# Moving the two requests for w_in from SyncE's DMA queue to ScalarE's

## The chip, the cores and the metric

The kernel runs on one NeuronCore of one Trainium2 chip. The core has five engines with one in-order instruction stream each: TensorE (PE, with its weight loads shown as PEld), VectorE (DVE), ScalarE (ACT), GpSimd (POOL) and SyncE (SP). Data come from HBM to the on-chip memory by DMA transfers. A transfer is asked for by an instruction in the stream of one engine, and the core's 16 DMA engines carry it out. The metric is the time of one execution on the device, in microseconds (us).

## The reference

Two stages. The first is a gated linear recurrence over 4 batches, 8 heads, 768 positions and a head size of 48. The second is a gated MLP over the 384 joined head outputs of each position, with a hidden width of 1024.

```python
for t in range(S):
    state = alpha[:, :, t, :, None] * state + np.einsum('bhd,bhe->bhde', k[:, :, t], v[:, :, t])
    y[:, :, t] = np.einsum('bhd,bhde->bhe', q[:, :, t], state)
...
h = np.maximum(x @ w_in, 0.0)                     # x: (4, 768, 384), w_in: (384, 1024)
u, v = (h[..., :d_ff // 2].copy(), h[..., d_ff // 2:].copy())
v_n = (v - mu) / np.sqrt(var + 1e-06)             # over the 512 columns of v
v_s = np.einsum('ts,bsd->btd', w_spatial, v_n) + b_spatial[None, :, None]
return ((u * v_s) @ w_out).astype(np.float32)
```

So w_in has two halves of 384 x 512 numbers: half 0 makes u, half 1 makes v. Each half is 768 KB in float32.

## The kernel before

**Stage one** works on chunks of 128 positions, 24 in all (6 per batch). The first 8 chunks (batch 0 and the first two of batch 1) are done in pairs by `pair` (lines 423 to 632), the rest one by one by `first` (lines 634 to 790). For each pair four loads of 384 KB bring `ac` (alpha), `kc`, `qc` and `vc` (line 441). They move rows of 96 numbers, 384 bytes. From `ac` ScalarE makes logarithms (`la`, line 452). TensorE adds them up (line 461). ScalarE makes the two exponentials (lines 469 and 478). These scale k (`kt`, line 483, on VectorE or GpSimd) and q (`qt`, line 490, on VectorE). TensorE transposes both (line 511), makes scores (line 583), and adds up the output from the masked scores (line 610) and from the running state (line 623). The output is turned into `xT`, the input of stage two.

**Stage two** has `second_v` (lines 867 to 940), which multiplies `xT` with half 1 of w_in, and normalizes. `second_u` multiplies with half 0. `second_s` multiplies with w_spatial, and `second_o` with w_out. All of their matmuls are recorded under the helper's line 828.

**Weights** come through `fetch` (lines 1073 to 1097): one DMA of 768 KB into one of two float32 buffers called `raw_w` (for w_in in rows of 512 numbers, 2 KB), and then casts to bfloat16. For each half of w_in there are three casts: two on GpSimd (line 199) and one on ScalarE (line 197). A third `raw_w` load, of w_spatial, can start only when the casts of half 1 have read their buffer, and the fourth only when those of half 0 have.

**The order of the work** is written out by hand in `PLAN`. Each word is an engine's letter (P, D, A, G, S for TensorE, VectorE, ScalarE, GpSimd, SyncE; Q marks a DMA's own time and issues nothing) and the number of an operation. `replay` (lines 111 to 120) emits the operations in this order, and each engine runs its own in order. A number behind a colon adds a matmul on junk data in front (line 187). The operations that matter here:

- S163, S165, S167, S169: the requests for `ac`, `kc`, `qc`, `vc` of the third pair (chunks 4 and 5). S307, S309, S311: `ac`, `kc`, `qc` of the fourth pair.
- S4 and S9: the requests for half 1 and half 0 of w_in (line 1081). Half 1 stands between `ac` and `kc` of the third pair, half 0 between `vc` of the third and `ac` of the fourth.
- A78: ScalarE's cast of the first chunk's output (`x_sb`, line 197). Next on ScalarE is A108, the cast of the second pair's `vc` (`vbp`).
- A171: ScalarE's logarithm of the third pair's `ac` (line 452). Next on ScalarE is A183, the first exponential of the third pair (line 469).
- A8, G7, G6: the casts of half 1. A13, G11, G12: those of half 0.

Of the kernel before, what the change touches and what calls it, by code (L numbers as in the profile page):

```python
# [61 lines left out]
Q308 P131 P134 D133 D136 D132 D135 G70 G118 P172:228 P182 P123:240 A183 A8 A173 A124 P137 P138 A139 A174 G7 G6 D125  # L62
P85 G126 D128 D185 G127 G129 G175 P88 P142 P140 A86 A184 D176 D186 A143 A89 P188 P190 P180 P144 P178 A141 A191 A145
A181 P146 G11 G12 S309 Q310 S311 Q312 D130 D87 D179 D90 D189 P157 A187 A177 A158 A147 A13 P197 P200 P192 D199 D201
D198 D194 D202 P151:196 P155 A315 A193 A91 P326 P316 A327 P203 P153 P204 G195 G196 G329 A317 A328 A318 P149 A205 A154
D159 D156 D152 D330 G319 P208 P334 A209 P206 D320 P332 P324 P210 P322 D92 D335 D325 D333 D148 A207 P212 A211 A150 P347
P215 P221 A213 A160 A222 A216 S14 Q15 P223 P227 S18 Q19 D93 D323 D161 D348 D349 D214 G16 G17 A224 A228 P225 P229 A226
A21 P232 A234 D231 D230 D233 G20 P235:300 P238 S313 Q314 G331 G321 P344 P336 S367 Q368 S369 Q370 S22 Q23 S371 Q372
A237 A236 D217 D162 D346 A240 D338 A239 A218 D219 D220 A375 A337 P251 P263 P259 P376 A377 A378 G339 P264 D345 D341
D265 P260 D261 P255 P252 A380 A25 A24 D381 D253 P256 D257 G340 G342 G379 S409 Q410 S373 Q374 S446 Q447 S411 Q412 S413  # L70
Q414 S415 Q416 S26 Q27 S480 Q481 S448 Q449 S482 Q483 S450 Q451 S484 Q485 P383 A385 A417 S452 Q453 S577 Q578 S486 Q487
S581 Q582 S579 Q580 S583 Q584 P244 P241 P350 A246 D384 D245 D242 D243 P390 P354 P418 D392 D391 A351 A355 G262 G343
A420 A382 G254 G266 P279 P352 P271 P356 P393 P272 A353 A357 A419 G421 A422 A394 P280 P361 P386 P275 P395 A362 A424
A396 A31 D273 D423 D281 D387 P425 D397 D427 D426 D363 G282 G388 P276 P358 D277 P398 G258 G389 G278 G30 A399 A454 A359
A28 A488 P405 P432 P267 P455 P401 A402 A457 A456 D29 P291 P489 P268 A490 A459 D406 D433 D400 D434 D360 P283 P428 D269
D460 A492 D429 D493 G458 G491 P435 A284 A292 A436 G274 G461 G270 G430 G431 S648 Q649 S617 Q618 S650 Q651 S611 Q612
S652 Q653 S613 Q614 S690 Q691 S615 Q616 S694 Q695 S654 Q655 S692 Q693 P287 P462 P437 P495 P403 D463 D464 D497 D496
A288 A439 A438 P440 A585 A441 A364 D404 P469 P498 P295 P465 P586 P303 D471 D470 D466 D500 D499 A296 A587 A588 A590
A304 P299 G494 G467 G468 G589 G592 D591 D442 P472 A473 P501 P407 P474 A502 A300 P503 P593 P596 A443 A505 A408 D475
D476 P477 A478 D504 D366 D594 D595 D445 D444 D597 D365 P506 P600 P515 D601 D516 A507 A479 A508 D509 D602 A656 A510  # L80
A619 P517 P525 P513 P519 P529 P657 P533 P620 D511 D512 P526 P530 A514 A659 A658 A621 A661 A622 A698 A624 D518 D520
D527 D531 D662 P545 P534 P699 A701 A700 A703 D625 G598 G599 G660 G626 G623 G528 D535 P546 D547 P630 P627 P664 P537
P603 D631 D665 D704 G548 A629 A628 G632 G663 A604 P538 P634 P605 S728 Q729 S762 Q763 S696 Q697 S730 Q731 S732 Q733
S764 Q765 S766 Q767 D539 A607 A666 A606 D635 D636 P541 P667 P542 G702 G532 P706 P671 D668 D543 D673 D672 G669 G536
G670 G544 G633 P608 P637 P521 A707 A736 A708 A638 P737 P713 P639 P522 P549 D714 D715 D641 D523 A770 A609 A705 A738
A739 G740 A640 A741 D742 P771 P550 P642 A772 P709 P744 A774 A643 A746 D710 D551 D775 D745 D644 G524 S858 Q859 S734
Q735 S929 Q930 S860 Q861 G773 G711 G552 G712 G743 G540 P716 P674 A717 A675 P561 P718 P676 P777 P553 A562 A678 A677
D719 D779 D720 D610 P679 P751 A778 A554 A866 A680 A645 A681 P780 D752 P747 D748 D753 D781 D782 P682 P867 P721 P754
A868 A869 A871 A722 A755 S768 Q769 S862 Q863 A723 A776 D683 D872 P573 P688 P684 G749 G750 G870 P756 P874 D646 D757
D875 D685 D758 A689 A574 D724 A876 P686 P783 P569 P881 A784 P785 A570 A787 A687 A725 D882 D786 D883 P759 P557 A760  # L90
P788 P565 P796 P798 P800 S1042 Q1043 S971 Q972 S892 Q893 S864 Q865 S898 Q899 S896 Q897 A979 A558 A789 A566 A937 A900
S894 Q895 S935 Q936 G873 S975 Q976 S931 Q932 S933 Q934 S973 Q974 S977 Q978 S1008 Q1009 S567 Q568 S1046 Q1047 S559 Q560
S1012 Q1013 S1010 Q1011 S1044 Q1045 S1014 Q1015 D727 D647 D761 D726 P794 P806 D790 A791 D799 D797 D795 D792 D793 D801
P901 P980 P802 P938 P877 P807 A902 A903 A907 A905 A981 A939 A940 A982 A944 A984 P810 P803 A942 G904 D878 G941 G879
D808 D906 D804 G805 G880 G809 G983 D985 D943 P822 P884 P811 D812 A885 P823 P908 P886 P945 D824 P814 P911 P815 D912
D909 D816 G813 G817 G913 G825 A910 A887 A888 A947 A946 P889 A1016 A890 P952 P915 P987 D953 D916 D954 P830 P1017 P831
P818 A988 A1019 A1050 A1018 D917 P948 P819 P1051 D949 A1021 A986 A989 D1022 D832 G950 P834 A1052 G951 G1020 P990 P842
P918 A835 A1054 D820 D991 D1055 A843 A919 P838 P1024 P994 P920 D1025 D921 D995 D996 A839 A1023 G914 G833 G1053 G992
S1048 Q1049 S575 Q576 S836 Q837 S844 Q845 S293 Q294 S289 Q290 S571 Q572 S305 Q306 S301 Q302 S555 Q556 A922 A1026 S297
Q298 S285 Q286 S840 Q841 P826 P955 P827 D828 A956 P1057 P957 P1031 D958 P1027 D1028 D1033 D1032 P997 P923 A1058 A1059  # L100
A959 P969 P1060 A1056 A998 P999 D1062 D1001 D1061 D970 G821 G829 G993 G1029 A1000 A924 P960 P846 P1034 A961 A847 G1030
P1063 A1035 A1064 P1002 P963 P1036 P1065 D925 D891 A1003 D962 D1066 P850 P967 A1067 A1037 D1004 A926 D928 P1068 A964
A1038 P1039 D927 D968 A851 A1005 A1069 A1040 D1006 D1041 D1007 D1070 P965 P854 P1076 P1080 P1078 P1074 D966 A1079 A855
A1071 A1081 D1075 D1072 D1073 D1077 P1094 P1082 P1106 P1086 P1083 P1098 P1095 P1090 P1102 P1087 P1107 P1091 P1103
# [19 lines left out]
def kernel(  # L124
# [946 lines left out]
    fetched, casts = [], []  # L1071

    def fetch(key, prio, to, src):

        n, cols = src.shape[1], src.shape[2]
        hold = {}

        def load(_):
# [2 lines left out]
            nc.sync.dma_start(out=hold["w"], in_=src)  # L1081
# [75 lines left out]
```

## Time and profile before

| what | value |
| --- | --- |
| time, median of 3 runs | 146.31 us (146.35, 144.73, 146.31) |
| span of the profiled execution, first to last instruction | 142.7 us (the profile gives this execution no other time) |
| busy, share of the span | PE 94%, DVE 83%, ACT 77%, POOL 58% |
| granted TensorE clock | 1.000 of full speed |
| request for half 1 of w_in | SP, 11.69 us, 8.3 us to landing |
| request for half 0 of w_in | SP, 19.86 us, 7.3 us to landing |
| ScalarE's A78 and A171 | 14.06 to 14.54 us and 17.33 to 18.18 us |

Times in the trace count from the start of the span. An engine counts as busy while an instruction of it runs. The time of a DMA request on SP's line is the time that the instruction held SP, not the time of the transfer. "To landing" goes from the start of the request to the arrival of the last byte.

### The profile page before, as it was taken

What the parts mean: (1) busy time and instruction counts of PE and PEld (TensorE: products, weight loads), DVE (VectorE), ACT (ScalarE), POOL (GpSimd) and SP (SyncE); (2) the same over time, 40 slices, a digit from 0 to 9 for tenths busy, and PEclk for the clock granted to TensorE, in tenths of its full rate; (3) what the DMA queues carried; (4) which work ended last, traced back from release to release, by engine and by line L of the source; (5) the groups of instructions that cost most, each with busy time, mean ns of one, the idle gap of its engine ahead of it and who ended that gap; (6) DMA issues with size and microseconds to landing.
All of it is one profiled execution on the core that took longest, in us unless ns stands there. A gap on an engine that the chain in (4) does not pass through costs nothing.

```text
span 142.7 us, 4968 instructions
## 1 busy us (share of the span) xinstructions
PE 134.7 (94%) x1912; PEld 84.8 (59%) x1923; DVE 118.3 (83%) x291; ACT 109.3 (77%) x282; POOL 83.4 (58%) x146
## 2 busy tenths in 40 slices
PE   7999798899999999999999999999999989999990
PEld 3457575566577656675666665656666656566560
DVE  7279878989989699999998898989979779994940
ACT  3477759999888969889987999997978978940061
POOL 6703977366339776982389999410799993000720
PEclk9999999999999999999999999999999999999999
DMA  4999999999998999999999998999998794113045
GB/s 106 270 261 261 321 259 256 290 289 358 236 217 160 237 226 202 194 169 203 171 196 183 182 198 140 214 152 194 191 231 165 229 341 168 56 58 111 0 161 170
DMA packets 89000, 28.64 MB, mean 201 GB/s; under 512 B 83728, under 2 KB 87440, under 8 KB 88976
## 3 DMA queue, kind: packets, MB, share of 16 engines
q1 hardware_dynamic: 88944, 28.32, 91.3%
q8 instruction: 15, 0.25, 0.8%
q14 instruction: 9, 0.07, 0.2%
q0 software_dynamic: 32, 0.00, 0.0%
HBM read 23.60 MB, written 4.72 MB: 198 GB/s over the span
## 4 chain that ended last, share of the span: by engine, by line
PE 63%; SPq 9%; POOL 7%; DMA 6%; DVE 5%; ACT 4%; issue 3%; ACTq 0%; POOLq 0%; DVEq 0%
PE bank L828 46%; SPq L441 8%; DMA qc<-in_q_dram 6%; PE bank L719 2%; PE bank L754 2%; POOL kt L690 2%; POOL gT L989 2%; POOL sbd L199 2%; PE bank L782 2%; DVE ptm L765 1%; PE bank L740 1%; PE bank L666 1%; SPq L1081 1%; PE bank L776 1%; DVE qt L490 1%
## 5 line engine op out<-in xcount | busy, mean ns | idle before, releaser
L828 PE MATMUL bank<-w_spT,vn 128*128 128x384 bf16 x192 | 36.8, 326 | 0.0
L989 POOL TENSOR_TENSOR gT<-vsb,uT 128x384 bf16<-128x384 f32 x28 | 25.7, 925 | 14.9 <-DVE vsb L976 14.4
L765 DVE TENSOR_TENSOR ptm<-bank,mask 128x512 bf16<-128x512 f32 x32 | 20.7, 682 | 1.9 <-PE bank L398 1.2
L828 PEld LDWEIGHTS <-vn 128*128 128x128 bf16 x192 | 16.6, 97 | 9.5 <-issue 0.2
L690 POOL TENSOR_TENSOR kt<-kc,binv 128x384 bf16<-128x384 f32 x16 | 14.6, 915 | 9.9 <-ACT bc L685 5.1
L976 DVE TENSOR_TENSOR vsb<-bank,bsp_bc 128x384 f32<-128x384 f32 x31 | 16.5, 551 | 4.2 <-PE bank L828 2.5
L828 PE MATMUL bank<-xT,w_in 128*128 128x384 bf16 x96 | 18.7, 326 | 0.0
L828 PE MATMUL bank<-w_out_sb,gT 128*128 128x384 bf16 (+1 forms) x100 | 18.7, 319 | 0.0
L828 PE MATMUL bank<-w_in,xT 128*128 128x512 bf16 x61 | 17.1, 379 | 0.8 <-issue 0.2
L344 POOL TENSOR_TENSOR state<-state,bc 128x192 f32<-128x192 f32 x20 | 10.4, 522 | 8.9 <-ACT bc L559 3.4
L197 ACT COPY kqT<-bank 128x512 bf16<-128x512 bf16 x21 | 12.1, 598 | 3.7 <-PE bank L719 1.1
L199 POOL CAST sbd<-state 64x192 bf16<-64x192 f32 x38 | 13.3, 350 | 2.0
L893 DVE BATCH_NORM_STATS2 stats<-v_sb 128x6 f32<-128x512 bf16 x20 | 13.6, 682 | 0.3 <-ACT v_sb L203 0.3
L203 ACT ACTIVATE v_sb<-bank 128x512 bf16<-128x512 f32 x20 | 11.7, 604 | 1.2 <-PE bank L828 1.0
L828 PEld LDWEIGHTS <-w_in 128*128 128x128 bf16 x96 | 8.8, 97 | 5.9
L828 PEld LDWEIGHTS <-gT 128*128 128x128 bf16 x100 | 8.9, 97 | 5.6 <-DVE gT L989 0.4
L199 DVE COPY kqT<-bank 128x512 bf16<-128x512 bf16 x27 | 10.4, 416 | 1.9 <-PE bank L511 1.0
L197 ACT CAST x_sb<-bank 128x384 bf16<-128x384 f32 x24 | 11.4, 489 | 0.7 <-PE bank L610 0.2
L187 PE MATMUL bank<-junk 128*128 128x512 f32 (+9 forms) x24 | 10.5, 542 | 1.1 <-DVE junk L240 1.1
L197 ACT COPY xT<-bank 128x192 bf16<-128x192 bf16 (+1 forms) x26 | 9.3, 376 | 1.7 <-PE bank L398 1.1
L594 DVE TENSOR_TENSOR ptm<-bank,mask 128x512 bf16<-128x512 f32 x16 | 10.2, 682 | 0.5 <-PE bank L583 0.3
L197 ACT COPY o_sb<-bank 128x384 f32<-128x384 f32 x9 | 4.4, 484 | 8.0 <-PE bank L828 8.0
(126 smaller groups left out, 285.4 us busy)
## 6 DMA issues: line engine op xcount, KB each, us to landing
ac<-in_alpha_dram SPq DMA_DIRECT2D x16, 192.0 KB, 4.4
kc<-in_k_dram SPq DMA_DIRECT2D x16, 192.0 KB, 4.9
qc<-in_q_dram SPq DMA_DIRECT2D x16, 192.0 KB, 4.3
vc<-in_v_dram SPq DMA_DIRECT2D x16, 192.0 KB, 4.4
raw_w<-in_moe_w_spatial_dram SPq DMA_DIRECT2D x3, 768.0 KB, 6.7
out_dram<-raw_w SPq DMA_DIRECT2D x11, 192.0 KB, 2.7
out_dram<-o_sb SPq DMA_DIRECT2D x9, 192.0 KB, 1.9
ac<-in_alpha_dram SPq DMA_DIRECT2D x4, 384.0 KB, 6.2
```

The source lines that it names most:

```text
L187: nc.tensor.matmul(out=flat[:, 0:cols].rearrange("p (a b) -> p a b", a=4), lhsT=junk, rhs=junk[:, None, 0:n].to_broadcast([128, 4, n]), st ...
L197: nc.scalar.copy(out=out, in_=in_)
L199: ENG[eng].tensor_copy(out=out, in_=in_)
L203: nc.scalar.activation(out=out, in_=in_, func=AF.Relu)
L344: ENG[eng].tensor_tensor(out=st["state"], in0=st["state"], in1=st["bc"][:, :, None].to_broadcast([128, HP, D]), op=ALU.mult)
L441: nc.sync.dma_start(out=t.rearrange("p h a d -> p h (a d)"), in_=src[b, :, t0:t0 + 2 * C, :].rearrange("h (p a) d -> p h (a d)", a=2))
L690: ENG[eng].tensor_mul(out=k_blocks(kt3)[:, :, :, 0:D], in0=quad(st["kc"]), in1=st["binv"])
L765: nc.vector.tensor_tensor(out=st["ptm"][:, s], in0=st[f"pt{s}"], in1=mask4, op=ALU.mult)
L828: return lambda ps: nc.tensor.matmul(out=out(ps), lhsT=lhsT(), rhs=rhs(), start=start, stop=stop)
L893: nc.vector.bn_stats(out=stats, in_=d["v_sb"][:, tt, :])
L976: nc.vector.tensor_tensor(out=hold["vs"], in0=ps[:, 0:TH], in1=bsp_bc[:, th, :], op=ALU.add)
L989: ENG[eng].tensor_tensor(out=bt[b]["gT"][:, dsl, cols], in0=hold["vs"], in1=bt[b]["uT"][:, dsl, cols], op=ALU.mult)
```

## The change

Both requests for w_in leave SyncE's stream and go into ScalarE's: half 1 behind A78, half 0 behind A171. They then go out on ScalarE's DMA queue. Buffers, sizes, casts and all other operations keep their places. The rest of `PLAN` is only wrapped anew.

```diff
 PLAN = """
 ...
-S163 Q164 S4 Q5 S165 Q166 S167 Q168 P59:464 G58 G48 A44 A45 A55 D46 D57 D47 P249:304 P49 P61 A50 P51 D52 D60 A62 A102
-A250 P71:304 P74 P113 P103 D72 D73 D76 D75 P63 P77:172 D65 A114 D116 P119:148 A104 A64 A115 A105 A78 G66 G67 G106 D107
-D117 D68 P79 P81 P111 P121 P247 P109 G3 G69 A108 A82 A80 D120 D122 D112 D110 P83 A84 A171 D248 S169 Q170 S9 Q10 S307
+S163 Q164 S165 Q166 S167 Q168 P59:464 G58 G48 A44 A45 A55 D46 D57 D47 P249:304 P49 P61 A50 P51 D52 D60 A62 A102 A250
+P71:304 P74 P113 P103 D72 D73 D76 D75 P63 P77:172 D65 A114 D116 P119:148 A104 A64 A115 A105 A78 A4 Q5 G66 G67 G106
+D107 D117 D68 P79 P81 P111 P121 P247 P109 G3 G69 A108 A82 A80 D120 D122 D112 D110 P83 A84 A171 A9 Q10 D248 S169 Q170
 ...
         def load(_):
             flat = raws.tile([128, n * cols], FP32, name="raw_w")
             hold["w"] = flat.rearrange("p (n f) -> p n f", n=n)
-            nc.sync.dma_start(out=hold["w"], in_=src)
-
-        dma(key, WT, load, list(fetched[-NRAW] if len(fetched) >= NRAW else []), prio, issue=0.68)
+            (nc.scalar if key[0] == "w_in" else nc.sync).dma_start(out=hold["w"], in_=src)
+
+        dma(key, WT, load, list(fetched[-NRAW] if len(fetched) >= NRAW else []), prio, "ACT" if key[0] == "w_in" else "SP",
+            issue=0.68)
```

More of the change, by code (lines that the diff above doesn't have):

```diff
@@ L63 @@
[L63 to L102, printed above, removed]
@@ L103 @@
-A1038 P1039 D927 D968 A851 A1005 A1069 A1040 D1006 D1041 D1007 D1070 P965 P854 P1076 P1080 P1078 P1074 D966 A1079 A855
-A1071 A1081 D1075 D1072 D1073 D1077 P1094 P1082 P1106 P1086 P1083 P1098 P1095 P1090 P1102 P1087 P1107 P1091 P1103
+S163 Q164 S165 Q166 S167 Q168 P59:464 G58 G48 A44 A45 A55 D46 D57 D47 P249:304 P49 P61 A50 P51 D52 D60 A62 A102 A250
+P71:304 P74 P113 P103 D72 D73 D76 D75 P63 P77:172 D65 A114 D116 P119:148 A104 A64 A115 A105 A78 A4 Q5 G66 G67 G106
+D107 D117 D68 P79 P81 P111 P121 P247 P109 G3 G69 A108 A82 A80 D120 D122 D112 D110 P83 A84 A171 A9 Q10 D248 S169 Q170
@@ new lines @@
+S307 Q308 P131 P134 D133 D136 D132 D135 G70 G118 P172:228 P182 P123:240 A183 A8 A173 A124 P137 P138 A139 A174 G7 G6
+D125 P85 G126 D128 D185 G127 G129 G175 P88 P142 P140 A86 A184 D176 D186 A143 A89 P188 P190 P180 P144 P178 A141 A191
+A145 A181 P146 G11 G12 S309 Q310 S311 Q312 D130 D87 D179 D90 D189 P157 A187 A177 A158 A147 A13 P197 P200 P192 D199
+D201 D198 D194 D202 P151:196 P155 A315 A193 A91 P326 P316 A327 P203 P153 P204 G195 G196 G329 A317 A328 A318 P149 A205
+A154 D159 D156 D152 D330 G319 P208 P334 A209 P206 D320 P332 P324 P210 P322 D92 D335 D325 D333 D148 A207 P212 A211 A150
@@ new lines @@
+P347 P215 P221 A213 A160 A222 A216 S14 Q15 P223 P227 S18 Q19 D93 D323 D161 D348 D349 D214 G16 G17 A224 A228 P225 P229
+A226 A21 P232 A234 D231 D230 D233 G20 P235:300 P238 S313 Q314 G331 G321 P344 P336 S367 Q368 S369 Q370 S22 Q23 S371
+Q372 A237 A236 D217 D162 D346 A240 D338 A239 A218 D219 D220 A375 A337 P251 P263 P259 P376 A377 A378 G339 P264 D345
+D341 D265 P260 D261 P255 P252 A380 A25 A24 D381 D253 P256 D257 G340 G342 G379 S409 Q410 S373 Q374 S446 Q447 S411 Q412
+S413 Q414 S415 Q416 S26 Q27 S480 Q481 S448 Q449 S482 Q483 S450 Q451 S484 Q485 P383 A385 A417 S452 Q453 S577 Q578 S486
@@ new lines @@
+Q487 S581 Q582 S579 Q580 S583 Q584 P244 P241 P350 A246 D384 D245 D242 D243 P390 P354 P418 D392 D391 A351 A355 G262
+G343 A420 A382 G254 G266 P279 P352 P271 P356 P393 P272 A353 A357 A419 G421 A422 A394 P280 P361 P386 P275 P395 A362
+A424 A396 A31 D273 D423 D281 D387 P425 D397 D427 D426 D363 G282 G388 P276 P358 D277 P398 G258 G389 G278 G30 A399 A454
+A359 A28 A488 P405 P432 P267 P455 P401 A402 A457 A456 D29 P291 P489 P268 A490 A459 D406 D433 D400 D434 D360 P283 P428
+D269 D460 A492 D429 D493 G458 G491 P435 A284 A292 A436 G274 G461 G270 G430 G431 S648 Q649 S617 Q618 S650 Q651 S611
@@ new lines @@
+Q612 S652 Q653 S613 Q614 S690 Q691 S615 Q616 S694 Q695 S654 Q655 S692 Q693 P287 P462 P437 P495 P403 D463 D464 D497
+D496 A288 A439 A438 P440 A585 A441 A364 D404 P469 P498 P295 P465 P586 P303 D471 D470 D466 D500 D499 A296 A587 A588
+A590 A304 P299 G494 G467 G468 G589 G592 D591 D442 P472 A473 P501 P407 P474 A502 A300 P503 P593 P596 A443 A505 A408
+D475 D476 P477 A478 D504 D366 D594 D595 D445 D444 D597 D365 P506 P600 P515 D601 D516 A507 A479 A508 D509 D602 A656
+A510 A619 P517 P525 P513 P519 P529 P657 P533 P620 D511 D512 P526 P530 A514 A659 A658 A621 A661 A622 A698 A624 D518
@@ new lines @@
+D520 D527 D531 D662 P545 P534 P699 A701 A700 A703 D625 G598 G599 G660 G626 G623 G528 D535 P546 D547 P630 P627 P664
+P537 P603 D631 D665 D704 G548 A629 A628 G632 G663 A604 P538 P634 P605 S728 Q729 S762 Q763 S696 Q697 S730 Q731 S732
+Q733 S764 Q765 S766 Q767 D539 A607 A666 A606 D635 D636 P541 P667 P542 G702 G532 P706 P671 D668 D543 D673 D672 G669
+G536 G670 G544 G633 P608 P637 P521 A707 A736 A708 A638 P737 P713 P639 P522 P549 D714 D715 D641 D523 A770 A609 A705
+A738 A739 G740 A640 A741 D742 P771 P550 P642 A772 P709 P744 A774 A643 A746 D710 D551 D775 D745 D644 G524 S858 Q859
@@ new lines @@
+S734 Q735 S929 Q930 S860 Q861 G773 G711 G552 G712 G743 G540 P716 P674 A717 A675 P561 P718 P676 P777 P553 A562 A678
+A677 D719 D779 D720 D610 P679 P751 A778 A554 A866 A680 A645 A681 P780 D752 P747 D748 D753 D781 D782 P682 P867 P721
+P754 A868 A869 A871 A722 A755 S768 Q769 S862 Q863 A723 A776 D683 D872 P573 P688 P684 G749 G750 G870 P756 P874 D646
+D757 D875 D685 D758 A689 A574 D724 A876 P686 P783 P569 P881 A784 P785 A570 A787 A687 A725 D882 D786 D883 P759 P557
+A760 P788 P565 P796 P798 P800 S1042 Q1043 S971 Q972 S892 Q893 S864 Q865 S898 Q899 S896 Q897 A979 A558 A789 A566 A937
@@ new lines @@
+A900 S894 Q895 S935 Q936 G873 S975 Q976 S931 Q932 S933 Q934 S973 Q974 S977 Q978 S1008 Q1009 S567 Q568 S1046 Q1047 S559
+Q560 S1012 Q1013 S1010 Q1011 S1044 Q1045 S1014 Q1015 D727 D647 D761 D726 P794 P806 D790 A791 D799 D797 D795 D792 D793
+D801 P901 P980 P802 P938 P877 P807 A902 A903 A907 A905 A981 A939 A940 A982 A944 A984 P810 P803 A942 G904 D878 G941
+G879 D808 D906 D804 G805 G880 G809 G983 D985 D943 P822 P884 P811 D812 A885 P823 P908 P886 P945 D824 P814 P911 P815
+D912 D909 D816 G813 G817 G913 G825 A910 A887 A888 A947 A946 P889 A1016 A890 P952 P915 P987 D953 D916 D954 P830 P1017
@@ new lines @@
+P831 P818 A988 A1019 A1050 A1018 D917 P948 P819 P1051 D949 A1021 A986 A989 D1022 D832 G950 P834 A1052 G951 G1020 P990
+P842 P918 A835 A1054 D820 D991 D1055 A843 A919 P838 P1024 P994 P920 D1025 D921 D995 D996 A839 A1023 G914 G833 G1053
+G992 S1048 Q1049 S575 Q576 S836 Q837 S844 Q845 S293 Q294 S289 Q290 S571 Q572 S305 Q306 S301 Q302 S555 Q556 A922 A1026
+S297 Q298 S285 Q286 S840 Q841 P826 P955 P827 D828 A956 P1057 P957 P1031 D958 P1027 D1028 D1033 D1032 P997 P923 A1058
+A1059 A959 P969 P1060 A1056 A998 P999 D1062 D1001 D1061 D970 G821 G829 G993 G1029 A1000 A924 P960 P846 P1034 A961 A847
@@ L105 @@
+G1030 P1063 A1035 A1064 P1002 P963 P1036 P1065 D925 D891 A1003 D962 D1066 P850 P967 A1067 A1037 D1004 A926 D928 P1068
+A964 A1038 P1039 D927 D968 A851 A1005 A1069 A1040 D1006 D1041 D1007 D1070 P965 P854 P1076 P1080 P1078 P1074 D966 A1079
+A855 A1071 A1081 D1075 D1072 D1073 D1077 P1094 P1082 P1106 P1086 P1083 P1098 P1095 P1090 P1102 P1087 P1107 P1091 P1103
 P1110 P1099 P1111 D1096 D1084 G1085 D1088 D1097 D1108 D1092 D1093 G1089 P1113 D1104 G1109 G1105 D1112 D1100 D1101
```

1 line of the change is left out of this document (removed).

## The prediction

> **What bounds the kernel now.** I read the page's busy shares first, then the chain that ended last in order of time, then the DMA requests around the change.
>
> ```profile
> PE 134.7 (94%) x1912; PEld 84.8 (59%) x1923; DVE 118.3 (83%) x291; ACT 109.3 (77%) x282; POOL 83.4 (58%) x146
> ...
> PE 63%; SPq 9%; POOL 7%; DMA 6%; DVE 5%; ACT 4%; issue 3%; ACTq 0%; POOLq 0%; DVEq 0%
> ```
>
> TensorE has 8 us of idle time in 142.7. A shift at the start has little to be lost in. The chain says where the start hangs:
>
> ```profile
> 11.69 1.67 SPq L1081
> 13.35 0.04 issue
> 13.40 0.52 SPq L441
> 13.92 0.04 issue
> 13.96 8.82 DMA qc<-in_q_dram
> 22.78 0.03 issue
> 22.83 0.04 issue
> 22.88 1.02 DVE qt L490 x2
> ```
>
> Start, length, what. Up to 22.8 us the chain is SP's requests and the landing of the third pair's `qc`. Behind that it holds no transfer, only engines. Are SP's requests slow, or are the DMA engines full? The requests from 11.6 to 15.6 us, with their time to landing, and below them three stretches of the span, whose last three columns are the granted clock, the DMA engines' busy share and GB/s:
>
> ```profile
> raw_w<-in_moe_w_in_dram SPq DMA_DIRECT2D x1, 768.0 KB, 8.3
> kc<-in_k_dram SPq DMA_DIRECT2D x1, 384.0 KB, 8.0
> qc<-in_q_dram SPq DMA_DIRECT2D x1, 384.0 KB, 8.8
> vc<-in_v_dram SPq DMA_DIRECT2D x1, 384.0 KB, 8.6
> ```
>
> ```profile
> 12.00:14.00 2.00, 1.96 (x76) 1.57 (x74) 2.00 (x5) 1.65 (x5) 0.17 (x1) 1.00 1.27 261
> 16.50:17.50 1.00, 0.61 (x19) 0.43 (x21) 1.00 (x4) 0.63 (x3) 0.93 (x4) 1.00 1.02 372
> 22.00:24.00 2.00, 1.66 (x16) 0.85 (x15) 1.64 (x5) 1.91 (x5) 1.88 (x4) 1.00 0.89 187
> ```
>
> Start plus time to landing gives half 1 of w_in at 20.0 us, `kc` 21.4, `qc` 22.8, `vc` 24.1. The request before them, `ac` at 10.25 with 6.3, landed at 16.5. So the transfers land in the order of the requests, one at a time: w_in 3.5 us behind its forerunner, the loads 1.4 us apart. 384 KB at the 261 GB/s of the first row is 1.5 us, SP's usual 1.44 us per request: the requests wait for the DMA engines, which are full. w_in runs faster (372 GB/s, 2.1 us for 768 KB); that it needed 3.5 us to land I read as one slow DMA engine of the sixteen. **The start is bound by the transfers in front of `qc`.**
>
> **The change, part by part.**
>
> *SP loses two requests* of 1.67 and 1.36 us. Its later requests are made earlier, and queue for the same full engines: worth nothing by itself, except that `qc`'s place in line moves up.
>
> *ScalarE gains two instructions.* No request by ScalarE is in this trace. The nearest rows are SP's: 0.55 us (a w_spatial request) and 0.76 us (w_out) when the queue has room, 1.36 and 1.67 us for w_in itself with a full queue. ScalarE's queue is empty, so I take 0.6. Below nothing it can't go: no instruction leaves ScalarE. The rows that cover it:
>
> ```profile
> 15.14 0.51 ACT L197 CAST vbp<-vc 128x384 bf16<-128x384 f32 x1 [0.60 <-DMA vc<-in_v_dram]
> ...
> 16.95 0.48 ACT L197 COPY xT<-bank 128x384 bf16<-128x384 bf16 x1 [0.37 <-PE bank L374]
> 17.33 0.85 ACT L452 ACTIVATE la<-ac 128x768 bf16<-128x768 f32 x1
> 19.27 0.49 ACT L469 ACTIVATE binvp<-bank 128x384 bf16<-128x384 f32 x1 [1.09 <-POOL sbd L199]
> ```
>
> The brackets are ScalarE's idle time before an instruction. The first request falls into the 0.60 us before `vbp`, the second into the 1.09 us before the exponential. Cost 0 at 0.6 us; at 1.67 us the first overruns by 1.1, of which the 0.37 us wait takes back a part, and the second by 0.3 at 1.36. Neither request waits for a semaphore (both `raw_w` buffers are fresh). Queued behind them stand the logarithm and the exponentials, which `kt` and `qt` need.
>
> *The transfers change places.* This is where I see the cost. Half 1 is asked for at 14.5 us and not at 11.7. The first load of the kernel was asked for at 0.74 us, and the stretch from 0 to 2 us moved 8 GB/s against 250 in the next: bytes flow about 1.2 us after a request. So half 1 flows from 15.7 us, near its old turn (behind `ac`, 16.5), but now beside `kc` and `qc`, not ahead of them. Half 0 is asked for at 18.2 us, not at 19.86 behind `vc`, so it flows from 19.4 us on: ahead of `qc`'s end, which it was behind. How two queues share a DMA engine this trace can't show, so I work out two ends:
> - *Piece by piece.* A load has 1024 pieces of 384 bytes, 64 on each DMA engine (1.5 us, 23 ns each); a half has 384 pieces of 2 KB, 24 on each (2.1 us, 88 ns each). In turns, w_in has four fifths of the time. Half 1 lands near 20.0 as before. Half 0 is through by 19.4 + 2.1 + 24 x 0.023 = 22.0 us, all ahead of `qc`, which lands at 22.8 + 2.1 = 24.9. `qt` starts 2.1 us late.
> - *Equal time.* Half 1 needs 4.2 us beside the loads, and the slow engine's 1.4 us more (3.5 - 2.1): its bytes end at 21.3, and it lands by some half us later, 1.8 us late. `qc` is late by about 1.0. But the casts of half 1 stand before the second exponential on ScalarE and before the state on GpSimd, and TensorE's `second_v` before the transposes of `kt` and `qt`: all shift by 1.8.
>
> The Trainium skill's page "DMA: Bandwidth & Descriptors", section "Queues, rings and completion order", says that a DMA engine takes the queues in turn, a packet at a time, of some 9 to 17 pieces. With as many pieces of each queue in a turn that is the first end, 2.1 us; no run here shows it yet.
>
> Either end gives about 2 us, because both half 1 and `qc` are needed by 22 us and half 0 is not: POOL waits 3.0 us for it, but TensorE first uses it at 28.6, behind the scores. The row of 22 to 24 us has some room (187 GB/s against 261: 0.6 us), in which half 0 could flow for nothing. I take **+1.9 us**, with 1.0 to 2.6 as the bounds of this case. Passing on: behind 22.9 us the chain has no transfer, and VectorE and TensorE hardly idle, so I let it pass whole. Gained back: VectorE's 0.33 us wait for `qc` and GpSimd's 0.57 for half 1 are what earlier landings could win at most.
>
> Sum against the profiled execution: 142.7 + 1.9 = 144.6 of span. The median of the runs is 3.6 us above this span, and I carry that: 146.3 + 1.9 = **148.2 us**.
>
> **Rivals.**
> 1. *ScalarE is held by its own requests.* SP makes requests with 0.04 us between them, from 3 to 27 us. If one unit serves both engines' requests, ScalarE's must wait for SP's running one, up to 1.44 us, and then need 1.67 and 1.36 with full engines. First request: 14.5 + 1.44 + 1.67 = 17.65, so `vbp` is 2.5 us late, and the logarithm 2.0 behind the 0.37 and 0.1 us waits. Second: 20.2 + 1.44 + 1.36 = 23.0, against the exponential's 19.27: +3.7, so 150.0 us. From 2.3 (waits half as long) to 5 (one SP request held 4.37 us). For it: every request here that found the engines full took over 1 us. Against: its queue is empty. The Trainium skill, "Perfetto Trace Analysis", section "DMA Instruction — HWDGE (DVE, Sync)", says the descriptor unit is locked for one request until its descriptors are made; by that this rival happens, if SP and ScalarE share the unit. No run here shows whether they do.
> 2. *Not slower: the queues overlap.* If a DMA engine works on one queue's 2 KB pieces while the other queue's small ones are handled, the loads run at w_in's rate beside it: two loads need 2 x 1.06 us in place of 2 x 1.5, so 0.9 us is won, and with the 0.6 us of room and the 0.33 us wait the 1.9 falls to about 0. It decides where the joint rate beside w_in exceeds 340 GB/s or so. Result: -0.4 to +0.9, near 146.3 us. For it: 372 GB/s shows the engines can. Against: it needs all three at once.
> 3. *The request is the limit*, as the chain names SP: `qc` is asked for 1.67 us sooner and lands so, 144.6 us. Against it is the 261 GB/s.
>
> **The numbers.** Forecast 0.55; rival 1, 0.22; rival 2, 0.20; rival 3, 0.03. Two per cent is 2.9 us, about what a measurement of this kernel can tell from no change. Slower than that: most of rival 1 and a tail of the forecast, 0.24. Faster than that: 0.03, for rival 3 and more. Within: 0.73. The range goes from 145.8 (rival 2's best) to 150.4 (rival 1 a little above its 3.7), which leaves out about 0.1 of rival 1 and rival 3; the forecast's own is 147.3 to 148.9.
>
> **What would show it.** Right: `qt` of the third pair or `second_v`'s first matmul starts 1 to 2.6 us late with a wait for a DMA before it; half 0 lands by 24 us; ScalarE's two requests take under 0.8 us. Rival 1: they take over 1.5 us, and `vbp` and the exponential are late. Rival 2: over 340 GB/s from 19 to 23 us, `qt` near 22.9. The prediction is wrong if a late start is made up behind 28 us, or if a TensorE stall near 24 us lowers the granted clock. Against that: before, TensorE is done at 139.4 us and the page keeps 9 to the end.

## The result, and the profile after

The changed kernel takes 146.78 us (median of 20 runs, 145.78 to 147.51), the kernel before 145.57 us beside it (20 runs, 144.20 to 146.93). The ratio is **1.0097, 95% interval 1.0069 to 1.0126**: about 1.2 to 1.4 us slower, less than the 2% that counts as a change here. The profiled execution took 146.89 us with a span of 145.1 us, so 1.8 us lie around the span. By the same 1.8 us, the profiled execution of before (span 142.7) took about 144.5 us, 1.1 below its median. Of the 2.4 us between the two spans, 1.1 is that luck. A ratio, here and below, leaves out runs more than 1.5% above the fastest run of their kernel.

The page's busy times and the DMA queues of the kernel after (packets, MB, share of 16 engines), and its shares of the chain:

```profile
PE 133.4 (92%) x1912; PEld 84.2 (58%) x1923; DVE 118.7 (82%) x291; ACT 108.9 (75%) x282; POOL 83.4 (58%) x146
...
q1 hardware_dynamic: 88144, 26.75, 83.5%
q10 hardware_dynamic: 800, 1.57, 3.2%
...
PE 65%; SPq 8%; DMA 8%; POOL 7%; DVE 4%; issue 3%; ACT 2%; ACTq 0%; POOLq 0%; DVEq 0%
```

Every engine does the work it did before. `q10` is new: ScalarE's queue, with the 1.57 MB of w_in. ScalarE has no more busy time than before (108.9 against 109.3), and its requests (ACTq) are no part of the chain. TensorE's idle time grew from 8 us to 11.7.

The chain of the kernel after, in order of time (start, length, what):

```profile
11.77 1.66 SPq L441
13.43 0.04 issue
13.47 11.53 DMA qc<-in_q_dram
25.00 0.03 issue
...
25.10 1.02 DVE qt L490 x2
```

The same piece as before carries the start: `qc` of the third pair. It is asked for 0.49 us sooner (13.47, not 13.96) and lands 2.2 us later, at 25.00. Behind it `qt` starts at 25.10, not at 22.88. Half 1 of w_in is late as well: it lands at 21.6, not at 20.0. TensorE in the timeline of the kernel after shows both, one after the other (the bracket is the idle time before the instruction and what ended it):

```profile
22.92 1.45 PE L828 MATMUL bank<-w_in,xT 128*128 128x512 bf16 x5 [2.18 <-POOL w_in L199]
24.45 0.33 PE L623 MATMUL bank<-sbd,kqT 128*128 128x96 bf16 x4
24.62 0.33 PE L374 MATMUL bank<-ident,x_sb 128*128 128x128 bf16 x3
25.71 0.38 PE L511 MATMUL bank<-ident,kt 128*128 128x128 bf16 x4 [0.76 <-DVE qt L490]
26.17 0.51 PE L511 MATMUL bank<-ident,qt 128*128 128x128 bf16 x6
```

Three of the same groups in the kernel before:

```profile
21.28 1.46 PE L828 MATMUL bank<-w_in,xT 128*128 128x512 bf16 x5
...
23.48 0.38 PE L511 MATMUL bank<-ident,kt 128*128 128x128 bf16 x4 [0.18 <-DVE qt L490]
23.95 0.62 PE L511 MATMUL bank<-ident,qt 128*128 128x128 bf16 x8
```

TensorE first waits 2.18 us for the casts of half 1 and falls 1.6 us behind, then 0.76 us more for `qt`, and is 2.2 us behind. Nothing makes it up: the first matmul on w_spatial starts at 42.6 (40.4 before), the last on w_out at 141.5 (139.1).

ScalarE's timeline after, with the two requests:

```profile
13.57 0.48 ACT L197 CAST x_sb<-bank 128x384 bf16<-128x384 f32 x1
13.57 0.42 ACTq L1081 DMA_DIRECT2D raw_w<-in_moe_w_in_dram  x1
15.18 0.51 ACT L197 CAST vbp<-vc 128x384 bf16<-128x384 f32 x1 [1.13 <-DMA vc<-in_v_dram]
...
16.66 0.37 ACTq L1081 DMA_DIRECT2D raw_w<-in_moe_w_in_dram  x1
16.88 0.85 ACT L452 ACTIVATE la<-ac 128x768 bf16<-128x768 f32 x1
18.78 0.49 ACT L469 ACTIVATE binvp<-bank 128x384 bf16<-128x384 f32 x1 [1.05 <-PE bank L461]
21.66 0.62 ACT L197 CAST w_in<-raw_w 128x512 bf16<-128x512 f32 x1 [2.39 <-DMA raw_w<-in_moe_w_in_dram]
```

The requests hold ScalarE 0.42 and 0.37 us. The logarithm (16.88, before 17.33) and the exponential (18.78, before 19.27) are not late. That they are earlier is no gain of the change: ScalarE is 0.3 us ahead of the first trace at 6 us already, before it makes a request. And the requests don't wait for the end of the instruction ahead of them: the first goes out with `x_sb` at 13.57, the second at 16.66, before the logarithm behind which it is written has begun, 0.03 us behind the landing of `ac` (16.63).

The DMA requests of the kernel after from 13.4 to 16.6 us (KB each, us to landing), and the bytes that moved in that stretch by queue:

```profile
q1 hardware_dynamic: 2190, 0.83, 124.5%
...
raw_w<-in_moe_w_in_dram ACTq DMA_DIRECT2D x1, 768.0 KB, 8.1
kc<-in_k_dram SPq DMA_DIRECT2D x1, 384.0 KB, 7.5
qc<-in_q_dram SPq DMA_DIRECT2D x1, 384.0 KB, 11.5
vc<-in_v_dram SPq DMA_DIRECT2D x1, 384.0 KB, 11.6
```

Half 1 is asked for at 13.57, and `q10` has no row: by 16.6 us no byte has moved on it. The first moves at 16.75, 3.2 us behind the request. Half 0 (asked for at 16.66) moves its first byte at 20.5, 3.8 us behind, when the last bytes of half 1, ahead of it on the same queue, move. It lands at 25.5 (27.2 before). So half 1 has moved behind `kc` (19.31, before 21.4), and half 0 ahead of the end of `qc` (25.00, before 22.8).

It is only this end that is late. A load has 1024 pieces of 384 bytes, and `qc` of the third pair is the eleventh load. By 21 us SyncE's queue had moved 10.95 loads' worth of such pieces, against 11.06 before (counted in the traces). The missing twentieth, some 50 pieces, is within the share of one DMA engine of the sixteen (64 pieces). So one late DMA engine, which moves half 0's pieces ahead of its last pieces of `qc`, would explain the landing; the trace doesn't name the engine of a piece.

### The profile page after: what moved, and what is told of

Same layout as the page of the kernel before. It is cut to its first block, busy times and chain, and to the rows that moved or that the text cites. A ratio compares the mean times of both kernels' runs of the same rounds, so it can differ in the third digit from the quotient of the medians.

```text
span 145.1 us, 4969 instructions
## 1 busy us (share of the span) xinstructions
PE 133.4 (92%) x1912; PEld 84.2 (58%) x1923; DVE 118.7 (82%) x291; ACT 108.9 (75%) x282; POOL 83.4 (58%) x146
## 3 DMA queue, kind: packets, MB, share of 16 engines
q10 hardware_dynamic: 800, 1.57, 3.2%
## 4 chain that ended last, share of the span: by engine, by line
PE 65%; SPq 8%; DMA 8%; POOL 7%; DVE 4%; issue 3%; ACT 2%; ACTq 0%; POOLq 0%; DVEq 0%
PE bank L828 47%; SPq L441 8%; DMA qc<-in_q_dram 8%; PE bank L719 2%; PE bank L754 2%; POOL kt L690 2%; POOL gT L989 2%; PE bank L740 2%; POOL sbd L199 2%; PE bank L666 2%; PE bank L782 2%; PE bank L776 1%; PE bank L398 1%; DVE stats L893 1%; PE bank L840 1%
## 5 line engine op out<-in xcount | busy, mean ns | idle before, releaser
L828 PE MATMUL bank<-w_spT,vn 128*128 128x384 bf16 x192 | 36.8, 326 | 0.0
L828 PEld LDWEIGHTS <-vn 128*128 128x128 bf16 x192 | 16.6, 97 | 9.5 <-issue 0.2
L976 DVE TENSOR_TENSOR vsb<-bank,bsp_bc 128x384 f32<-128x384 f32 x31 | 16.5, 551 | 4.2 <-PE bank L828 2.5
L828 PE MATMUL bank<-w_in,xT 128*128 128x512 bf16 x61 | 17.1, 379 | 2.9 <-POOL w_in L199 2.2
L828 PE MATMUL bank<-xT,w_in 128*128 128x384 bf16 x96 | 18.7, 326 | 0.0
L828 PE MATMUL bank<-w_out_sb,gT 128*128 128x384 bf16 (+1 forms) x100 | 18.7, 319 | 0.0
L203 ACT ACTIVATE v_sb<-bank 128x512 bf16<-128x512 f32 x20 | 11.7, 597 | 2.6 <-PE bank L828 2.5
L828 PEld LDWEIGHTS <-w_in 128*128 128x128 bf16 x96 | 8.8, 97 | 5.9
L828 PEld LDWEIGHTS <-gT 128*128 128x128 bf16 x100 | 8.9, 97 | 5.6 <-DVE gT L989 0.4
L187 PE MATMUL bank<-junk 128*128 128x512 f32 (+9 forms) x24 | 9.9, 513 | 1.1 <-DVE junk L240 1.1
L828 PEld LDWEIGHTS <-xT 128*128 128x128 bf16 x72 | 6.0, 97 | 8.0 <-issue 2.3
```

Source lines behind the costliest of these rows:

```text
L203: nc.scalar.activation(out=out, in_=in_, func=AF.Relu)
L828: return lambda ps: nc.tensor.matmul(out=out(ps), lhsT=lhsT(), rhs=rhs(), start=start, stop=stop)
L976: nc.vector.tensor_tensor(out=hold["vs"], in0=ps[:, 0:TH], in1=bsp_bc[:, th, :], op=ALU.add)
```

## The experiments

**The theories.** The first, called O where an expectation names it by a letter: the *places in time* of the transfers decide. Half 1 is late because it moves later, `qc` because half 0 moves ahead of it. The rivals: ScalarE loses time through its own requests; a second queue is slow, or slows the first, whatever the places; a dip of the granted TensorE clock makes the loss. A further one, L, came up on the way: the loss has two sizes, by when `ac` lands.

The experiments differ from the kernel before by the diffs shown. Their `PLAN` is wrapped in one line less, so in most of their traces line numbers are one less than before (L827 for L828, L489 for L490); with the two small requests they differ more. Each ratio is to runs of the kernel before on the same chip.

### The kernel before once more

> The kernel before once more, for a second trace of it. In the first, the third pair's qc landed at 22.8 us and half 1 of w_in at 20.0. If that trace was typical, both land within 0.3 us of this here. If the first trace was a lucky one (its run took 144.5 us where the median is 145.6), one of them lands about 1 us later.

144.24 us, span 142.5. `qc` lands at 22.66 and half 1 at 19.89, as in the first trace. But the third pair's `ac` lands at 17.79 and not at 16.5, so that the logarithm waits 1.11 us for it, and the time is none the longer. In this execution of the kernel before, `ac` lands 1.3 us later at no cost.

### Half 1 alone on ScalarE

```diff
-S163 Q164 S4 Q5 S165
+S163 Q164 S165
...
-A105 A78 G66
+A105 A78 A4 Q5 G66
...
-            nc.sync.dma_start(out=hold["w"], in_=src)
+            (nc.scalar if key == ("w_in", 1) else nc.sync).dma_start(out=hold["w"], in_=src)
```

> Only half 1 goes to ScalarE's queue; half 0 stays on SyncE behind vc of the third pair. Theory O (the loss is in the places that the transfers take among the others): half 1 lands 1.6 us late as with the full change, qc lands no later than 22.8, second_v and all behind it are late by 1.0 to 1.6 us: 146.6 to 147.2 us, against 145.6 before. Rival Q (a second queue costs by itself, whichever transfer is on it): qc lands late too, by about 1 us. Rival A (ScalarE is held by the request): vbp of the second pair starts later than 15.2.

146.30 us (6 runs), ratio 1.0104 [1.0052, 1.0155]; span 144.1. Half 1 lands at 21.71, `qc` at 22.82 as before. `second_v` starts at 22.99 (21.28 before) after 1.48 us of waiting for the casts, and `qt` at 24.18. Half 1 alone costs what the whole change costs by the medians, and `qc` has no part in it: `qt` is late because the second exponential stands behind ScalarE's cast of half 1.

### Half 0 alone on ScalarE

```diff
-A84 A171 D248 S169 Q170 S9 Q10 S307
+A84 A171 A9 Q10 D248 S169 Q170 S307
...
-            nc.sync.dma_start(out=hold["w"], in_=src)
+            (nc.scalar if key == ("w_in", 0) else nc.sync).dma_start(out=hold["w"], in_=src)
```

> Only half 0 goes to ScalarE's queue; half 1 stays on SyncE in its old place. Theory O: half 1 lands at 20.0 and half 0 passes qc, which lands near 25 and not at 22.8: 1.2 to 2.2 us slower, 146.8 to 147.8 us. Rival (only half 1's delay matters, qc's is hidden behind it): within 0.5 us of before.

Median 147.13 us of 12 runs, from 144.26 to 147.52, in no one cluster: six at 147.28 to 147.52, one at 146.98, three at 146.1 to 146.3, and 145.01 and 144.26. All twelve have their median 2.3 us above that of before (144.87); the ratio, 1.005 [0.9992, 1.0107], is that of the five shortest alone. The profile is of one of the long ones (span 145.6). `ac` lands at 16.42, half 0 is asked for at 16.46 and lands at 24.96, and `qc` lands at 24.80. VectorE and TensorE in its timeline:

```profile
24.89 1.02 DVE L489 TENSOR_TENSOR qt<-qc,bank 128x384 bf16<-128x384 f32 x2 [2.60 <-DMA qc<-in_q_dram]
...
22.72 0.33 PE L373 MATMUL bank<-ident,x_sb 128*128 128x128 bf16 x3
25.50 0.38 PE L510 MATMUL bank<-ident,kt 128*128 128x128 bf16 x4 [2.45 <-DVE qt L489]
```

Here `second_v` runs on time, so TensorE's whole wait falls in one piece of 2.45 us. The busy times by stretch behind it; the number ahead of the last two is the granted TensorE clock:

```profile
25.00:26.00 1.00, 0.41 (x5) 0.24 (x5) 0.97 (x3) 0.00 (x0) 0.99 (x2) 1.00 1.12 228
26.00:27.00 1.00, 1.00 (x12) 1.00 (x13) 0.97 (x3) 0.54 (x1) 0.18 (x1) 0.59 1.06 274
27.00:28.00 1.00, 1.00 (x8) 0.69 (x7) 0.81 (x4) 0.84 (x3) 0.00 (x0) 0.50 0.82 176
28.00:29.00 1.00, 1.00 (x4) 0.30 (x2) 0.96 (x4) 0.99 (x3) 0.00 (x0) 0.50 1.09 278
29.00:30.00 1.00, 1.00 (x11) 0.28 (x13) 0.18 (x1) 0.02 (x1) 0.00 (x0) 0.70 0.95 272
```

After the wait the clock is halved for 3.4 us. So half 0's early request can delay `qc`, and did so here; by the spread of the times, not in every run.

### Both on ScalarE, in other places

```diff
-S163 Q164 S4 Q5 S165
+S163 Q164 S165
...
-D65 A114 D116
+D65 A114 A4 Q5 D116
...
-A183 A8 A173
+A183 A8 A9 Q10 A173
...
-S169 Q170 S9 Q10 S307
+S169 Q170 S307
...
-            nc.sync.dma_start(out=hold["w"], in_=src)
+            (nc.scalar if key[0] == "w_in" else nc.sync).dma_start(out=hold["w"], in_=src)
```

> Both halves go out on ScalarE's queue, but at about the times at which SyncE asked for them before: half 1 behind A114, the first exponential of the second pair (near 11.6 us), half 0 behind A8, the cast of half 1 on ScalarE (near 20 us). Theory O: within 0.6 us of before (145.0 to 146.2), since half 1 lands by 20 us and half 0 behind qc. Rivals Q and A: 1.0 us slower or more, like the full change, since the queue and ScalarE's two requests are the same.

145.27 us (12 runs), ratio 0.9995 [0.9957, 1.0033] for nine of them: as fast as before, though both requests are ScalarE's. Half 1 is asked for at 11.54 (11.69 before) and lands at 20.36; half 0 is asked for at 20.39 (19.86 before) and lands at 28.0. `qc` lands at 22.86 and `qt` starts at 22.95. **In these nine runs, ScalarE as the issuer, and its queue, cost nothing that can be measured.** The other three took 147.4 to 147.9 us, at mean clocks of 0.988, 0.974 and 0.973. What they met isn't known; one run of before on this chip took 147.69 us at 0.986. The median of all twelve is 0.4 us above that of before (144.87).

### SyncE's line alone, half 1 later

```diff
-S163 Q164 S4 Q5 S165 Q166 S167
+S163 Q164 S165 Q166 S4 Q5 S167
```

> No request on ScalarE: SyncE keeps both, but asks for half 1 one place later, behind kc of the third pair, where the full change's trace has it. Theory O: half 1 lands near 21.4 in place of 20.0, qc stays near 22.8, second_v's first matmul comes 1.4 us late: 0.8 to 1.5 us slower than before. If the loss needs a second queue (rival Q): within 0.4 us of before.

145.65 us (12 runs), ratio 1.0064 [1.0033, 1.0095]; span 143.9. That is 0.6 us above before by the medians (145.04), 0.9 by the ratio. It is less than half 1 alone cost on ScalarE (1.4 and 1.5), but the intervals of the two ratios overlap. With no request on ScalarE, half 1 lands at 21.49 and `qc` at 22.84, and TensorE waits as in the changed kernel:

```profile
22.77 1.46 PE L827 MATMUL bank<-w_in,xT 128*128 128x512 bf16 x6 [2.26 <-POOL w_in L198]
```

### SyncE's line alone, half 0 sooner

```diff
-S165 Q166 S167
+S165 Q166 S9 Q10 S167
...
-S169 Q170 S9 Q10 S307
+S169 Q170 S307
```

> No request on ScalarE: SyncE asks for half 0 ahead of qc and vc of the third pair. Theory O: half 1 lands at 20.0 as before, qc 2.1 to 3.1 us later than 22.8, qt waits for it: 1.6 to 2.8 us slower than before. Rival Q: within 0.4 us.

147.33 us (6 runs, 146.92 to 147.55), ratio 1.0164 [1.0121, 1.0206]; span 145.7. `qc` is now behind half 0 in one queue (they land at 24.98 and 23.42), and all six runs are long. TensorE and VectorE in its timeline, the same wait as in the profile of half 0 on ScalarE, and the clock halved again (26.67 to 30.08 us):

```profile
25.68 0.38 PE L510 MATMUL bank<-ident,kt 128*128 128x128 bf16 x4 [2.50 <-DVE qt L489]
...
25.08 1.02 DVE L489 TENSOR_TENSOR qt<-qc,bank 128x384 bf16<-128x384 f32 x2 [2.65 <-DMA qc<-in_q_dram]
```

The last three experiments together decide for the first theory, against ScalarE's time and against the queue: with ScalarE and its queue, but in other places, nine of twelve runs show no loss; without them, in these places, there is one. A cost of the second queue of less than about 0.5 us, the upper end of the interval of both in other places, would not show.

### Two small requests on ScalarE

Two requests of 6 KB each in the places of the change, into buffers that nothing reads; w_in stays on SyncE. This is work added to the kernel.

```diff
+    def probe(n):
+        nc.scalar.dma_start(out=probes[n], in_=moe_w_in.rearrange("(ks p) f -> p ks f", p=128)[:, :, 4 * n:4 * n + 4])
...
+            if i == 0:
+                probe(0)
...
+            if j == 2:
+                probe(1)
```

> The kernel before with two more requests on ScalarE, in the two places of the change, for 6 KB each (128 x 3 x 4 numbers of w_in, in pieces of 16 bytes, into buffers that nothing reads). All other work is as before. They have the count of pieces of a half, so ScalarE's own cost is in, and the bytes are not. Theory O: within 0.4 us of before; each request holds ScalarE under 0.6 us. Rival A: 0.8 us slower or more. It also tells how long a request on an empty queue waits behind what SyncE has asked for: 2 to 2.5 us to landing if the queues take turns piece by piece, 4 us or more if it stands in line behind the earlier requests.

144.88 us (12 runs), ratio 1.0009 [0.9973, 1.0046]: two requests by ScalarE cost nothing that shows. They hold it 0.44 and 0.37 us. They also measure the queue. The requests from 13.2 to 17.0 us, and the queues that moved bytes in that time (`q10` has no row):

```profile
q1 hardware_dynamic: 1897, 1.11, 117.6%
...
probe<-in_moe_w_in_dram ACTq DMA_DIRECT2D x2, 6.0 KB, 6.4
```

6 KB on a queue with nothing else on it take 7.1 and 5.7 us to land. The first request, made at 13.37, moves no byte until 17.43. So the wait is not that of a large transfer. Of the expectation's two cases, 2 to 2.5 us or 4 and more, it is the second, which stands for a request in line behind what SyncE has asked for.

### Half 0 one instruction later

```diff
-S169 Q170 S9 Q10 S307
+S169 Q170 S307
...
-P123:240 A183 A8
+P123:240 A183 A9 Q10 A8
...
-            nc.sync.dma_start(out=hold["w"], in_=src)
+            (nc.scalar if key == ("w_in", 0) else nc.sync).dma_start(out=hold["w"], in_=src)
```

> Half 1 stays on SyncE in its place; half 0 goes out on ScalarE's queue one instruction later than in the full change, behind A183, the first exponential of the third pair (near 18.8 us). Bytes flowed 3.2 and 3.8 us after ScalarE's requests in the full change, so they start near 22.5 here, when qc is nearly through. Theory O: qc lands by 23.4, within 0.6 us of before, and at best 0.4 faster. Rival Q: 1 us slower or more.

144.57 us (12 runs), ratio 0.9993 [0.9956, 1.003]. Half 0 is asked for at 19.79, the time it had on SyncE, and lands at 26.36; `qc` lands at 22.73. Equal to before. The request that SyncE is rid of is worth nothing, and neither is half 0 landing 0.8 us sooner.

### Half 0 alone on ScalarE, with junk matmuls in the wait

Two junk matmuls are added ahead of P188 (the transposes of `kt` and `qt`), so that TensorE doesn't idle there.

```diff
-A143 A89 P188 P190
+A143 A89 P188:512:512 P190
```

> The kernel with only half 0 on ScalarE's queue, plus two matmuls on junk data (512 columns each, about 1 us each) on TensorE ahead of the transposes of the third pair's kt, where TensorE stood idle for 2.5 us in that kernel's trace and its clock was halved for 3.4 us behind. Theory O with clock: qc lands as late as there (near 24.9), the clock stays at 1.000 and the time falls by about 1 us, from 147.1 to 146.1. Rival (the late qc alone makes the 2.3 us): 147.1 as without the junk.

Six runs: 145.47, 145.48, 147.17, 147.64, 149.14, 149.30 us; ratio 1.011 [1.0024, 1.0197], without the last two. The profile caught an execution without the wait: `ac` lands at 17.80, half 0 is asked for at 17.83, and `qc` lands at 22.75 (clock 1.000). So on the clock it settles nothing. By their mean clocks, the two runs near 145.5 and those at 147.17 and 147.64 were at 1.000, the two above 149 at 0.985. If `qc` was late in the runs at 147, they speak for the rival, since they are as long at full clock as half 0 alone was at 0.986 to 0.988 (146.98 to 147.52); they weren't profiled. But the profile shows one way in which half 0 alone has more than one time: with `ac` 1.4 us later, its request is 1.4 us later, and `qc` is through in time. It isn't that half 0 as a whole moves later: its first byte moves at 20.36 us here, and at 20.40 in the long execution of half 0 alone. What differs is the end of `qc`. From 21 to 22 us SyncE's queue moves 43 pieces here, beside ScalarE's 173, and 13 beside 181 there.

### The whole change, with junk matmuls in the wait

Two junk matmuls are added ahead of P85 (`second_v`'s first matmuls) to the changed kernel.

```diff
-D125 P85 G126
+D125 P85:512:464 G126
```

> The full change plus two junk matmuls (512 and 464 columns) on TensorE ahead of second_v's first group, where it stood idle for 2.2 us. Seven of the twenty runs of the full change had a mean clock of 0.988, and 146.9 us against 146.5 for the others. Theory O with clock: no run at 0.988, and 0.2 to 0.4 us less than the full change beside it. Rival (no part of the loss is clock): the same as the full change.

146.84 us (6 runs), ratio 1.013 [1.007, 1.0189]. The junk runs from 21.04 to 22.9 us and fills the wait; `ac` lands at 16.50 and `qc` at 24.88; the mean clock is 0.996 in the profiled run. One of the six runs still had a mean clock of 0.986. The kernel is no faster than the changed kernel on the same chip (next). So idling TensorE and its clock are not shown to be a part of the whole change's loss.

### The whole change once more

> The full change once more, on the chip of the two others: 1.0 to 1.6 us slower than before, half 1 near 21.6 and qc between 24 and 25 us.

146.30 us (12 runs, 145.47 to 146.71), ratio 1.0106 [1.0071, 1.0141]; the profiled run took 145.86 us with a span of 144.1. This execution is of the other kind, with `qc` in time, against the expectation. ScalarE's timeline, and TensorE's:

```profile
17.93 0.84 ACT L452 ACTIVATE la<-ac 128x768 bf16<-128x768 f32 x1 [1.15 <-DMA ac<-in_alpha_dram]
17.93 0.38 ACTq L1081 DMA_DIRECT2D raw_w<-in_moe_w_in_dram  x1
```

```profile
22.92 1.45 PE L828 MATMUL bank<-w_in,xT 128*128 128x512 bf16 x5 [1.52 <-POOL w_in L199]
...
25.38 0.62 PE L511 MATMUL bank<-ident,qt 128*128 128x128 bf16 x8 [0.21 <-DVE qt L490]
```

The request for half 0 stands behind the logarithm, and the logarithm waits for `ac`: 17.90 here, 16.63 in the first trace. So half 0 is asked for at 17.93, `qc` keeps its time (22.79), and only half 1 is late (21.64). The transposes of `qt` start at 25.38: 1.4 us behind before, as the span is, and not the 2.2 of the first trace.

### Half 0 alone on ScalarE, two instructions sooner

```diff
-A82 A80 D120
+A82 A80 A9 Q10 D120
...
-S169 Q170 S9 Q10 S307
+S169 Q170 S307
...
-            nc.sync.dma_start(out=hold["w"], in_=src)
+            (nc.scalar if key == ("w_in", 0) else nc.sync).dma_start(out=hold["w"], in_=src)
```

> Half 1 on SyncE in its place; half 0 on ScalarE's queue behind A80 (the copy of xT, near 15.8 us) and not behind A171, the logarithm, which waits for ac of the third pair. In the traces so far ac landed at 16.4 to 16.6 us or at 17.8 to 18.0, half 0 was asked for right behind it, and qc landed at 24.8 to 25.0 in the first kind and at 22.8 in the second. Theory L (the spread from run to run comes through ScalarE's wait for ac, which sets when half 0 is asked for): here half 0 always passes qc, qc lands near 24.8 or later whenever ac lands, and all runs are slow, 146.8 to 147.6, none under 146. Rival (the spread is in the DMA engines whatever the request's time): runs under 145.5 remain, as with A171 (144.3 to 147.5).

147.15 us (6 runs, 147.01 to 147.43), ratio 1.0191 [1.015, 1.0232]. With the request ahead of the logarithm (15.26 us), no wait for `ac` stands before it, and the spread of half 0 alone (144.3 to 147.5) is gone: all six runs are long. `qc` lands at 24.81, and here `kc` is late too (23.65, before 21.43). TensorE in its timeline, with the clock halved from 25.04 to 28.45 us:

```profile
25.51 0.58 PE L510 MATMUL bank<-ident,kt 128*128 128x128 bf16 x4 [2.49 <-DVE qt L489]
```

Over all traces in which half 0 is on ScalarE: asked for at 15.26, 16.46, 16.66 or 16.95 us, `qc` lands at 24.8 to 25.0; asked for at 17.83, 17.93, 19.79 or 20.39 us, at 22.7 to 22.9. L holds in all eight. Why `ac` lands at 16.5 in one execution and at 17.9 in another, in the kernel before too, wasn't tried and stays open.

## Why the prediction was right, and where it was not

**Sign and size.** The forecast was +1.9 us, within 2%, in a range from 145.8 to 150.4 us. Measured are 146.78 us and +1.2 to 1.4 us. (The lower bound was rival 2's best, which by the working's own -0.4 is 145.9.) Of the 1.4 us between 148.2 and 146.78, 0.7 is the base (146.31 from three runs, 145.57 from twenty), and 0.7 the size of the one term. The 3.6 us carried between span and median was not a fixed cost: 1.8 us lie around the span, and the rest was the quick execution that was profiled.

**What bounds the start: right.** The transfers in front of `qc` do, not SyncE's requests. SyncE is rid of two requests, and most of its next ones hold it longer instead: `kc` of the third pair 1.66 us (0.52 before), the fourth pair's `ac` 3.27 (0.89) and `kc` 3.53 (0.75); only `vc` of the third is shorter (2.66, before 4.37). `qc`, asked for 0.49 us sooner, lands later. Rival 3 is out.

**ScalarE's cost of nothing: right.** 0.42 and 0.37 us, against the 0.6 taken, and nothing late behind them. Rival 1, that one unit serves both engines' requests in turn, would have had them over 1.5 us; SyncE was making requests at that moment (from 13.47 to 14.91 and from 14.95 on), so the lock that the Trainium skill's "Perfetto Trace Analysis", section "DMA Instruction — HWDGE (DVE, Sync)", describes held nothing up here. The small requests alone measure 1.0009. One reason given for this rival was misread: "every request here that found the engines full took over 1 us" isn't so in the working's own lines, where that for `kc` at 13.40 took 0.52 us.

**When the requests go out: mis-sized.** The working had 14.5 and 18.2 us, behind the end of the instructions ahead of them. They went out at 13.57 and 16.66, beside them.

**"Bytes flow about 1.2 us after a request": wrong.** That was taken from the first load, with idle DMA engines. With SyncE's earlier requests under way it is 3.2 and 3.8 us, and 4.1 for 6 KB. With the earlier requests it partly cancels: half 1's first bytes move at 16.75 (worked out: 15.7) and half 0's at 20.5 (19.4), both 1.1 us later than thought. So one of the signs named for being right failed: half 0 was to land by 24 us, and landed at 25.5. That of `qt`, 1 to 2.6 us late behind a DMA, and that of the requests, under 0.8 us, came true.

**The two ends: one held, the other matched by luck.** Half 1 lands 1.6 us late, near the second end's 1.8. But that end's reason, an equal share of the time with the loads, is wrong here. From 17 to 19 us ScalarE's queue had 93% of the DMA engines' time and moved 322 of its pieces, SyncE's 157. Half 1 isn't moved slower than before, only later: its first bytes move at 16.75 us, and at 15.26 in the kernel before, and from there to landing it takes 4.9 us, before 4.7. That `second_v` and `qt` shift with it did hold. `qc` lands 2.2 us late where half 0 gets ahead of its end: the first end's 2.1, 24 pieces of 88 ns on a DMA engine. There, from 21.5 to 22.5 us, the queues moved as many pieces each (columns: packets, MB, share; ScalarE's queue first):

```profile
q10 hardware_dynamic: 150, 0.31, 85.4%
q1 hardware_dynamic: 148, 0.06, 20.9%
```

In this stretch it is what the Trainium skill's "DMA: Bandwidth & Descriptors", section "Queues, rings and completion order", has as turns between queues, and with pieces of 2 KB against 384 bytes it gives w_in four fifths of the time, as worked out. In the last experiment it is so too (295 and 297 pieces from 20 to 22 us). But equal counts don't hold throughout: 322 stand against 157 above, and 181 against 13 in the profile of half 0 alone on ScalarE (21 to 22 us). Why one queue moves nearly alone there, the runs don't show. By itself the rule says nothing of the 3 to 4 us before the first piece.

**Rival 2** (the queues overlap, and all is hidden) is out: it needed over 340 GB/s from 19 to 23 us. The changed kernel moved 333 there, too near for the rate alone to decide; but `qt` starts at 25.1 us and not near 22.9.

**What the working missed: half 0's place hangs on `ac`.** It took one time for the request, 18.2 us. The request stands behind an instruction that waits for a transfer, and so inherits the spread of that transfer. The loss has a constant part, half 1 (span +1.4 us in the execution where it is alone, and 1.0104 for half 1 alone), and an occasional one, half 0 ahead of `qc` (span +2.4 us with both). They don't add up: TensorE needs both, and what is later decides. The forecast of 1.9 lies between the two, which is in part luck.

**"A late start is made up", "a stall lowers the clock".** The first did not happen in either trace of the change. The second did for half 0 alone and for half 0 sooner on either queue, where the wait is one piece of 2.5 us. In the changed kernel it is cut into 2.18 and 0.76 us, and the clock stayed at 1.00 from 22 to 30 us of the profiled run. Seven of its twenty runs had a mean clock of 0.988, which is what one halving of 3.4 us in 145 gives (1 - 1.7/145), and they took 146.94 us in the mean against 146.58 for the other thirteen. The same comparison shows nothing in the whole change once more (146.26 for five runs at 0.988, 146.13 for the other seven) or with half 1 alone (146.27 for four, 146.45 for two). What share of the loss is clock stays open: the runs with junk matmuls didn't settle it.

## What to carry to other kernels

When DMA engines are full, a request's place in time among the others decides, and hardly the queue that it goes out on: find the transfer that the chain waits for, and count what would come to stand ahead of it, and which other transfer would land later than its user needs it. A request put into a compute engine's in-order stream takes on the waits of the instructions ahead of it, so one that must not pass, or fall behind, another transfer should not stand behind an instruction with a wait of its own. And a single profiled execution may be a quick one: what lies around its span has to be known before its distance to the median is carried along.

## What was unexpected of the hardware

- *A request waits as long on ScalarE's empty queue as on SyncE's busy one.* Half 1, asked for at 11.54 us on ScalarE's queue (both in other places), moves its first byte at 15.46; at 11.69 on SyncE's (before), at 15.26. Half 0, asked for at 19.79 on ScalarE's queue (half 0 one instruction later), moves its first at 22.02; at 19.86 on SyncE's (before), at 22.08. So it is not the queue that makes a request of the change late; what makes all of them wait isn't shown.
- *ScalarE makes a DMA request beside a running activation*: 13.57 us for both `x_sb` (0.48 us long) and the request behind it in order.
- *With 2.5 us of TensorE idling came 3.4 us at half clock* in three kernels (26.18 to 29.59, 26.67 to 30.08, 25.04 to 28.45 us; the last begins before the idling ends at 25.51). The start of the half clock lies in each of them 20.48 us, six times 3.41, behind the first rise of the clock (5.70, 6.19, 4.56). That it goes by fixed stretches of 3.41 us, so that an idle time counts by where it falls in them, fits all three; no run tested it.
- *A 384 KB load lands at 16.4 to 16.6 or at 17.8 to 18.0 us* (`ac` of the third pair) in executions of the same kernel, with nothing between in the fourteen traces.
